# Attention-times-V of two head pairs in one excursion, their last keys as quarters of the array, two transposes moved earlier, fewer output buffers

## The chip, the cores and the metric

The kernel runs on one core of one Trainium2 chip. The metric is device time in microseconds (us), and each time quoted below for a whole kernel is a median over several executions; spans, stages and waits are read from one profiled execution. Before the change it was 528.9 us (three runs, 528.81 to 530.1). The profiled runs had a mean granted TensorE clock of 0.997 or more of full speed.

Names: PE is the TensorE matmul engine and PEld its weight loads, DVE is VectorE, ACT is ScalarE, POOL is GpSimd. PSUM is the memory into which PE accumulates; it is divided into banks, and each tile named `f` in the profile is one bank.

## The reference

```python
# q, k, v: (8, 12, 448, 64) fp32
scores = scale * (q @ k^T)                     # per batch and head, 448 x 448
attn   = maximum(scores, 0) ** 2 / 448
x      = attn @ v                              # heads side by side: (8, 448, 768)
xn     = (x - mean) / sqrt(var + 1e-6) * g_ln
out    = x + maximum(xn @ w_ch1, 0) @ w_ch2    # d_ff = 3072
```

## The kernel before

Matmuls are in bf16. The kernel works on one batch after another. While the first layer of the feed-forward of batch b runs (24 products of 12 matmuls, in halves of 64 output channels), the attention of batch b+1 is slipped in between its products as *excursions*, so that the engines that evict the scores (copy them out of PSUM) and square them have time.

Heads are handled in pairs (`i` counts pairs, 6 to a batch). The 448 keys are three tiles of 128 (`NF = 3`) and a rest of 64 (`SS`). The rest tiles of two neighbouring pairs share one tile, `attn[i, NF]` with even `i`, and its score matmuls use 64x64 quarters of the array.

The PSUM banks:

```python
sc    # 2 tiles of 2 banks: scores, evicted by ScalarE
fb    # 4 single banks
next_f = Turns(fb[:2]).next     # first-layer products AND attention-times-V take turns here
spare  = fb[2:]                 # the third score tile of an excursion, means
```

Attention-times-V (AV) of one pair goes into one bank, with eight matmuls (four tiles, two heads). The rest tile's half of V has zero rows, so all eight have the same 128x64 form:

```python
def att_AV(i, half=None, bank=None, evac_by=None):
    ...
        av[0] = (next_f() if bank is None else bank)[:, :S]
    ...
    order = [NF, 0, 1, 2] if i % 2 else [0, 1, 2, NF]
    # ... 8 matmuls into ps ...
    if evac_by is nc.scalar:
        nc.scalar.mul(xT_of(b, pr), ps, c2)                                 # eviction
    else:
        nc.vector.tensor_scalar(xT_of(b, pr), ps, c2, None, op0=Alu.mult)   # eviction
    # ... and an addition xs += xT on VectorE, for the mean
```

An excursion, and the places where it stands:

```python
def excursion(n, third=(nc.vector, nc.vector), **how):
    flush_loads()
    next_AV(**how)                              # one AV, if one is ready
    took = [slots.pop(0) for _ in range(n)]     # then n = 3 score tiles
    for m, (i, t) in enumerate(took):
        att_QK(i, t, relu_by=third if m == 2 else nc.scalar)
    for i, t in took:
        att_square(i, t)                        # VectorE, three squares
    ...
def ffn_1(ni):
    ps = next_f()[:, :S]
    # ... 12 matmuls ...
    nc.scalar.activation(h[:, ni, CARRY:], ps, Act.Relu)
# batches 1 to 6: an excursion after every third first-layer product
# (in batch 1 with evac_by=nc.scalar)
```

At the start, batch 0's own attention runs alone. Its last pair, the last two mean products (`mean_part`) and the first first-layer product on centred inputs (`ffn_1_first`) follow one another with little else to fill the gaps. The q and k of batch 1 are transposed on PE, five pairs of them inside batch 0's first layer (`T_IN_FIRST`).

## Time and profile before

| | before |
|---|---|
| median time | 528.9 us |
| span of the profiled run | 525.9 us |
| PE busy | 98% |
| chain of waits, share of PE | 81% |
| first-layer stage of batches 2 to 6, each | 37.72 us |
| first-layer stage of batch 0, batch 1 | 40.77, 39.58 us |

A *stage* here runs from its first first-layer matmul to the first second-layer matmul, by the start times of the records.

From the page of before, the span, the busy time of each engine, the granted clock in 40 slices (9 is 90% or more), and the chain that ended last, as shares of the span:

```profile
span 525.9 us, 13704 instructions
...
PE 517.0 (98%) x5705; PEld 309.9 (59%) x5705; DVE 375.3 (71%) x662; ACT 272.8 (52%) x444; POOL 221.8 (42%) x255
...
PEclk9999999999999999999999999999999999999999
...
PE 81%; DMA 12%; POOL 3%; DVE 2%; ACT 1%; issue 1%; POOLq 0%; DVEq 0%; ACTq 0%
```

TensorE bounds the kernel. To cost an edit one has to see how tightly its matmuls follow each other. The next fence is from the timeline of before, in the middle of a batch. Columns: start, duration (both us), engine, line, operation, output and input tile, shape, number of instructions, and in brackets the idle time before, with what ended it.

```profile
310.38 0.92 PE L319 MATMUL f<-at,v_ring 128*64 128x448 bf16 x8
310.65 0.54 ACT L399 ACTIVATE h<-f 128x448 bf16<-128x448 f32 x1 [0.65 <-PE f L397]
...
311.23 0.55 PE L284 MATMUL sc<-qkT_t 64*128 64x448 bf16 x4
311.42 0.62 DVE L326 TENSOR_SCALAR xT<-f 128x448 bf16<-128x448 f32 x1 [1.24 <-PE f L319]
...
311.72 0.38 PE L279 MATMUL f<-qkT_t 64*64 64x448 bf16 x4
...
312.03 3.60 PE L397 MATMUL f<-xc,w 128*64 128x448 bf16 x36
...
313.45 1.69 DVE L295 TENSOR_TENSOR at<-at 128x896 bf16<-128x896 bf16 x3
...
315.46 0.92 PE L319 MATMUL f<-at,v_ring 128*64 128x448 bf16 x8
```

Durations of matmul groups overlap the next group, because each record's end is modelled and lies about 0.35 us after its start. So one reads from start to start: 36 first-layer matmuls take 315.46 - 312.03 = 3.43 us, that is 0.19 us per pair of 128x64 halves. The AV's four pairs take 0.76 us, and to the next start it is 0.85, so the change of array tiling costs about 0.09. The AV (310.38) takes the one bank of the two, the latest first-layer product has the other. That product's ReLU runs from 310.65 to 311.19, and PE wants its bank only at 312.03, 0.84 us later. There is no hole in PE's work here.

### The profile page before, as it was taken

Reading aid. Unit: us, or ns where it says so; the run is one execution under the profiler, and the core shown is the slowest. Engines: PE = TensorE matmul, PEld = TensorE weight load, DVE = VectorE, ACT = ScalarE, POOL = GpSimd, SP = SyncE. Lnnn points to the kernel's source line nnn. Section 1 sums busy time; section 2 is a strip of 40 time slices with the busy share of each in tenths; the row PEclk is TensorE's granted clock in tenths of the full one; section 3 lists DMA queues with packets and bytes.
Section 4 is the critical chain, followed back from the end, with each engine's and each line's share of the span. In section 5 each row is a group of like instructions: output and inputs, shape, how many; then the busy total and the mean of one; then the engine's idle time right before and its main releaser. Section 6 shows DMA issues by size and latency. Waiting matters only on the chain.

```text
span 525.9 us, 13704 instructions
## 1 busy us (share of the span) xinstructions
PE 517.0 (98%) x5705; PEld 309.9 (59%) x5705; DVE 375.3 (71%) x662; ACT 272.8 (52%) x444; POOL 221.8 (42%) x255
## 2 busy tenths in 40 slices
PE   8989999999999999999999999999999999999996
PEld 4445566556765566655666556655666556665665
DVE  5967778778858869589584886788695876951265
ACT  6965551878236662366623666466524665234320
POOL 8628215676622683227732267428632000320021
PEclk9999999999999999999999999999999999999999
DMA  9999999999637993679934799769944200250022
GB/s 135 173 194 201 205 201 146 202 125 105 82 80 99 106 102 62 122 73 115 94 66 105 72 113 122 108 62 123 82 77 106 49 14 3 62 112 11 1 61 62
DMA packets 175230, 53.04 MB, mean 101 GB/s; under 512 B 154176, under 2 KB 175168, under 8 KB 175168
## 3 DMA queue, kind: packets, MB, share of 16 engines
q0 software_dynamic: 103552, 25.74, 55.3%
q1 hardware_dynamic: 71088, 26.06, 27.1%
q8 instruction: 44, 0.72, 0.6%
q10 hardware_dynamic: 528, 0.37, 0.2%
q14 instruction: 18, 0.15, 0.1%
HBM read 51.91 MB, written 11.01 MB: 120 GB/s over the span
## 4 chain that ended last, share of the span: by engine, by line
PE 81%; DMA 12%; POOL 3%; DVE 2%; ACT 1%; issue 1%; POOLq 0%; DVEq 0%; ACTq 0%
PE f L397 36%; PE f L459 34%; DMA w<-in_moe_w_ch_dram 6%; PE f L319 5%; DMA s_sb<-in_v_dram 4%; PE sc L284 3%; PE f L284 1%; DMA w<-in_k_dram 1%; DVE w L210 1%; POOL w L201 1%; PE sc L279 1%; ACT at L292 1%; POOL w L141 1%; PE f L356 0%; POOL w L144 0%
## 5 line engine op out<-in xcount | busy, mean ns | idle before, releaser
L397 PE MATMUL f<-xc,w 128*64 128x448 bf16 x2256 | 226.9, 354 | 0.7 <-DVE o_t L428 0.4
L397 PEld LDWEIGHTS <-w 128*64 128x64 bf16 x2256 | 124.6, 110 | 94.4 <-issue 19.1
L399 ACT ACTIVATE h<-f 128x448 bf16<-128x448 f32 x188 | 102.5, 545 | 102.6 <-PE f L397 101.1
L459 PE MATMUL f<-w,s_sb 128*64 128x384 bf16 (+2 forms) x1584 | 130.0, 324 | 0.0
L292 ACT ACTIVATE at<-sc 128x896 bf16<-128x896 f32 x120 | 103.4, 917 | 16.5 <-PE sc L284 13.3
L459 PEld LDWEIGHTS <-s_sb 128*64 128x64 bf16 x1584 | 89.6, 110 | 37.7
L295 DVE TENSOR_TENSOR at<-at 128x896 bf16<-128x896 bf16 x168 | 95.8, 618 | 5.1 <-ACT at L292 4.8
L166 POOL DMA_DIRECT2D qk_ring<-in_q_dram x36 | 47.0, 1305 | 95.4 <-DMA qkT_t<-qk_ring 85.9
L493 POOL TENSOR_TENSOR o_t<-o_t,x_tok 128x384 f32<-128x384 f32 x26 | 24.4, 938 | 146.6 <-ACT o_t L492 132.1
L290 DVE TENSOR_SCALAR at<-f 128x448 bf16<-128x448 f32 x89 | 51.6, 618 | 24.2 <-PE f L284 24.2
L453 DVE TENSOR_TENSOR s_sb<-h 128x1536 bf16<-128x1536 bf16 x65 | 64.8, 1014 | 0.0
L492 ACT ACTIVATE o_t<-f,rstd 128x384 f32<-128x384 f32 x26 | 15.1, 580 | 94.7 <-DVE acc L497 46.7
L167 POOL DMA_DIRECT2D qk_ring<-in_k_dram x36 | 55.2, 1533 | 9.3 <-DMA w<-in_moe_w_ch_dram 9.3
L459 PE MATMUL f<-w,h 128*64 128x384 bf16 x624 | 52.9, 326 | 0.0
L168 POOL DMA_DIRECT2D qk_ring<-in_k_dram x36 | 46.6, 1293 | 5.2 <-DMA w<-in_moe_w_ch_dram 5.2
L326 DVE TENSOR_SCALAR xT<-f 128x448 bf16<-128x448 f32 x43 | 26.7, 620 | 28.2 <-PE f L319 27.6
L459 PEld LDWEIGHTS <-h 128*64 128x64 bf16 x624 | 35.5, 110 | 15.5
L319 PE MATMUL f<-at,v_ring 128*64 128x448 bf16 x336 | 40.3, 354 | 0.5 <-DVE xT L326 0.2
L493 POOL TENSOR_TENSOR acc<-acc,x_tok 128x384 f32<-128x384 f32 x24 | 28.0, 1176 | 22.5 <-ACT acc L492 22.5
L363 DVE SCALAR_TENSOR_TENSOR xc<-f,g_sb,xc 128x448 bf16<-128x448 f32 x45 | 28.5, 678 | 6.4 <-PE f L356 6.0
L178 POOL DMA_DIRECT2D v_ring<-in_v_dram x36 | 32.3, 1202 | 0.0
L284 PE MATMUL sc<-qkT_t 64*128 64x448 bf16 x206 | 31.3, 356 | 0.0
(81 smaller groups left out, 381.1 us busy)
## 6 DMA issues: line engine op xcount, KB each, us to landing
w<-in_moe_w_ch_dram POOLq DMA_DIRECT2D x6, 768.0 KB, 12.7
w<-in_moe_w_ch_dram POOLq DMA_DIRECT2D x4, 1152.0 KB, 26.2
v_ring<-in_v_dram POOLq DMA_DIRECT2D x21, 192.0 KB, 5.4
qk_ring<-in_q_dram POOLq DMA_DIRECT2D x36, 112.0 KB, 4.7
qk_ring<-in_k_dram POOLq DMA_DIRECT2D x36, 96.0 KB, 5.2
out_dram<-o_t SPq DMA_DIRECT2D x9, 168.0 KB, 2.2
out_dram<-o_t SPq DMA_DIRECT2D x9, 144.0 KB, 2.1
out_dram<-acc SPq DMA_DIRECT2D x7, 144.0 KB, 2.0
```

What stands on the lines that cost most here:

```text
L166: nc.gpsimd.dma_start(q_to, q[b, heads].rearrange("x (p j) d -> p j x d", j=NJ))
L167: nc.gpsimd.dma_start(k_to[:, :NF], k[b, heads, :SF].rearrange("x (p t) d -> p t x d", t=NF))
L284: nc.tensor.matmul(by_j(half[hh]), k_of(i, r, t, P), q_of(i, r), start=True, stop=True)
L290: nc.vector.tensor_scalar(at[:, x], half[x], 0.0, None, op0=Alu.max)
L292: nc.scalar.activation(at, ps[:, :, :S], Act.Relu)
L295: nc.vector.tensor_mul(attn[i, t], attn[i, t], attn[i, t])
L319: nc.tensor.matmul(ps[hh * D:(hh + 1) * D, :], weights, values, start=(n == 0), stop=(n == NF))
L397: nc.tensor.matmul(ps[c * D:(c + 1) * D, :], w1[:, ki, n0:n0 + D], xc[:, ki, :], start=(ki == 0), stop=(ki == K1 - 1))
L399: nc.scalar.activation(h[:, ni, CARRY:], ps, Act.Relu)
L453: nc.vector.tensor_tensor(s_sb[:, n], x, y, op=op)
L459: nc.tensor.matmul(ps[c * D:(c + 1) * D, :d1 - d0], stat[:, ki, c * D:(c + 1) * D], w2[:, slot, ki, d0:d1], start=(start and ki == 0), sto ...
L493: nc.gpsimd.tensor_tensor(o_t, o_t, x_half(m, dh), op=Alu.add)
```

## The change

Three ideas, all meant to give PE less work or to fill its gaps.

1. AV of pairs `i` and `i+1` go into one excursion (a *joint*). Their rest tiles no longer cost two zero-padded pairs of 128x64 matmuls (0.38 us): the four 64x64 quarters run at once, in the time of one pair. The score tile that follows a joint is a rest tile in quarters too, so no further change of tiling is added. There are 14 joints, two in each of batches 0 to 6; the excursion before each goes without an AV.
2. Two of the transposes of batch 1's q and k leave batch 0's first layer for the gaps around the last two mean products.
3. The output buffers shrink (`acc` 4 to 3, `o` 3 to 2), and the attention tiles grow from 7 to 9, which the later AV needs.

```diff
+    def att_AV2(i, evac_by=None):
+        ps = [next_f()[:, :S] for _ in range(2)]
+        for x in range(2):
+            for t in range(NF):
+                av_part(ps[x], i + x, t, t == 0, False)      # three full tiles each
+        # ...
+        for x in range(2):
+            for hh in range(2):
+                r0 = row0(i + x, hh)                          # quarters
+                nc.tensor.matmul(ps[x][hh * D:(hh + 1) * D, :], v_rest[r0:r0 + SS, pr + x, r0:r0 + D],
+                                 attn[i, NF][r0:r0 + SS, x, :], start=False, stop=True)
+        for x in range(2):
+            av_out(i + x, ps[x], evac_by)
# ... in the slots:
+        if i % NPAIR == 4:
+            first[1:] = [(i, NF), (i, 1), (i, 2)]
# ... in excursion():
-        next_AV(**how)
+        if len(ready) > 1:
+            att_AV2(ready.pop(0), **how)
+            ready.pop(0)
+        elif ready and ready[0] % NPAIR == NPAIR - 2:
+            next_AV(**how)
# ... in step_fine(), for the last pairs: the square ahead of the AV's second half
# ... in first_end():
         att_AV(i - 1, 1)
+        att_T(i + 1, nc.scalar.copy, next_f())
         mean_part(i - 1)
+        att_T(i + 2, nc.scalar.copy, spare[1])
# ... in ffn_1_first():
-        tiles = [t[:, :S] for t in (f_ps, m_ps, spare[1], next_sc()[:, 0])]
+        tiles = [t[:, :S] for t in (f_ps, m_ps, next_sc()[:, 0], spare[1])]
...
-    T_IN_FIRST = {4: 1, 7: 2, 10: 3, 13: 4, 16: 5}
+    T_IN_FIRST = {10: 3, 13: 4, 16: 5}
# ... and batch 1's q and k of heads 2 to 5 are loaded before the first weight chunk
# ... buffers: attn 7 -> 9, acc 4 -> 3, o 3 -> 2
```

More of the change, by code (lines that the diff above doesn't have):

```diff
@@ L57 @@
     t_pool = ctx.enter_context(tc.tile_pool(name="qkT", bufs=3))
-    attn_pool = ctx.enter_context(tc.tile_pool(name="attn", bufs=7))
+    attn_pool = ctx.enter_context(tc.tile_pool(name="attn", bufs=9))
     st_pool = ctx.enter_context(tc.tile_pool(name="stats", bufs=4))
-    acc_pool = ctx.enter_context(tc.tile_pool(name="acc", bufs=4))
-    o_pool = ctx.enter_context(tc.tile_pool(name="o", bufs=3))
+    acc_pool = ctx.enter_context(tc.tile_pool(name="acc", bufs=3))
+    o_pool = ctx.enter_context(tc.tile_pool(name="o", bufs=2))
     ps_pool = ctx.enter_context(tc.tile_pool(name="ps", bufs=1, space=bass.MemoryType.PSUM))
@@ L248, in k_of, with att_T @@
         return flat(i)[r, c0:c0 + keys]
-    def att_T(i, copy=None):
+    def att_T(i, copy=None, bank=None):
         if i >= PE_T * NPAIR:
@@ L262, in att_T @@
             return
-        ps = bf_view(next_f() if i <= NPAIR else next_spare())
+        if bank is None:
+            bank = next_f() if i <= NPAIR else next_spare()
+        ps = bf_view(bank)
         for t in range(2):
@@ L302, in xT_of, with av_part @@
         return xT[:, ki, (b % 2) * S:(b % 2 + 1) * S]
+    def av_part(ps, i, t, start, stop):
+        b, pr = divmod(i, NPAIR)
+        v_heads, v_rest = v_parts(b)
+        for hh in range(2):
+            if t < NF:
+                weights, values = v_heads[:, 2 * pr + hh, t * D:(t + 1) * D], attn[i, t][:, hh, :]
+            else:
+                weights, values = v_rest[:, pr, row0(i, hh):row0(i, hh) + D], attn[i - i % 2, NF][:, i % 2, :]
+            nc.tensor.matmul(ps[hh * D:(hh + 1) * D, :], weights, values, start=start, stop=stop)
     def att_AV(i, half=None, bank=None, evac_by=None):
-        b, pr = divmod(i, NPAIR)
         if half != 1:
@@ L308, in att_AV, with av_out @@
         ps = av[0]
-        v_heads, v_rest = v_parts(b)
         order = [NF, 0, 1, 2] if i % 2 else [0, 1, 2, NF]
         for n, t in enumerate(order):
-            if half is not None and n // 2 != half:
-                continue
-            for hh in range(2):
-                if t < NF:
-                    weights, values = v_heads[:, 2 * pr + hh, t * D:(t + 1) * D], attn[i, t][:, hh, :]
-                else:
-                    weights, values = v_rest[:, pr, row0(i, hh):row0(i, hh) + D], attn[i - i % 2, NF][:, i % 2, :]
-                nc.tensor.matmul(ps[hh * D:(hh + 1) * D, :], weights, values,
-                                 start=(n == 0), stop=(n == NF))
-        if half == 0:
-            return
+            if half is None or n // 2 == half:
+                av_part(ps, i, t, n == 0, n == NF)
+        if half != 0:
+            av_out(i, ps, evac_by)
+    def att_AV2(i, evac_by=None):
[3 more added lines that the diff above has]
+                av_part(ps[x], i + x, t, t == 0, False)
+        b, pr = divmod(i, NPAIR)
+        v_rest = v_parts(b)[1]
+        for x in range(2):
+            for hh in range(2):
+                r0 = row0(i + x, hh)
[3 more added lines that the diff above has]
+            av_out(i + x, ps[x], evac_by)
+    def av_out(i, ps, evac_by):
+        b, pr = divmod(i, NPAIR)
         if evac_by is nc.scalar:
@@ L412, in new_o, with new_acc @@
         return o_t
+    def new_acc():
+        acc_t = acc_pool.tile([P, HD], fp32, tag="acc")
+        return acc_t
     def store(o_t, m, d0, d1, engines=(nc.sync,)):
@@ L444, in plain_part @@
         if part == parts - 1:
-            o_t = acc_pool.tile([P, HD], fp32, tag="acc")
+            o_t = new_acc() if dh else new_o()
             scaled_plus(o_t, box[m], m, x_half(m, dh))
@@ L476, in seven @@
         bb = c
-        acc1 = acc_pool.tile([P, HD], fp32, tag="acc")
-        acc2 = acc_pool.tile([P, HD], fp32, tag="acc")
+        acc1, acc2 = new_acc(), new_acc()
         tt = nc.vector.tensor_tensor
@@ L552, in after @@
                 def after(ps=ps, d0=d0, d1=d1):
-                    o_t = new_o()[:, :d1 - d0]
-                    scaled_plus(o_t, ps[:, :d1 - d0], m2, acc2[:, d0:d1])
+                    o_t = acc2[:, d0:d1]
+                    scaled_plus(o_t, ps[:, :d1 - d0], m2, o_t)
                     store(o_t, m2, HD + d0, HD + d1, (nc.sync, nc.scalar))
@@ L581 @@
             first[2:] = first[:1:-1]
-        slots += first + [(i + 1, t) for t in range(NF)]
+        second = [(i + 1, t) for t in range(NF)]
+        if i % NPAIR == 4:
+            first[1:] = [(i, NF), (i, 1), (i, 2)]
+        slots += first + second
     slots = slots[slots.index((NPAIR, 2)):]
@@ L588, in ends @@
         if i % 2 == 0:
-            return [i] if t == (NF - 1 if i % NPAIR == 2 else NF) else []
+            return [i] if t == (NF - 1 if i % NPAIR else NF) else []
         return [i] if t == NF - 1 else []
@@ L597, in excursion @@
         flush_loads()
-        next_AV(**how)
+        if len(ready) > 1:
+            assert ready[0] % 2 == 0 and ready[1] == ready[0] + 1
+            att_AV2(ready.pop(0), **how)
+            ready.pop(0)
+        elif ready and ready[0] % NPAIR == NPAIR - 2:
+            next_AV(**how)
         took = [slots.pop(0) for _ in range(n)]
@@ L640, in step_fine @@
             mean_part(i - 1)
-        att_AV(i, 1)
-        att_square(i + 1, 2)
+        if i + 2 < NPAIR:
+            att_AV(i, 1)
+            att_square(i + 1, 2)
+        else:
+            att_square(i + 1, 2)
+            att_AV(i, 1)
     def first_end():
@@ L783 @@
         load_heads(1, [("q", 0, 2), ("k", 0, 2), ("k last", 0, H)])
+        load_heads(1, [("q", 2, 4), ("k", 2, 4)])
         load_w1(0)
-        load_heads(1, [("q", 2, 4), ("k", 2, 4)])
         load_w1(1)
```

## The prediction

> **What bounds it.** TensorE. The page has PE busy 98% of 525.9 us, granted clock full; the chain of waits is 81% PE. In batches 2 to 6 the timeline shows PE without holes: 36 first-layer matmuls start 3.43 us apart from the next stage (0.19 us per pair of 128x64 halves), AV takes 0.76 us (four pairs), a change of array tiling costs 0.09 to 0.13 us. (The Trainium skill, "TensorEngine Tiling (Array Packing)", Key Properties, says that changing the mode drains the engine; the trace agrees, with those numbers.) From AV to AV an excursion lasts 4.96 or 5.08 us. PE is stalled elsewhere: 0.7 us before the last mean product, 0.8 us before the first centred product, and some tenths per excursion in batch 1 (ScalarE late).
>
> **Removed.** Two AV of a joint excursion take 6 pairs plus one set of four quarters (four 64x64 score matmuls go out in 0.19 us) instead of 8 pairs: -0.19 us, 14 times, -2.7 us. No tiling change is added, since quarter scores now follow directly. Two transposes leave the first-layer loop, 0.61 us each: -1.2 us.
>
> **Added, by the order of instructions.**
> (a) The second AV takes the PSUM bank that the first-layer product just before used. Its ReLU ends 0.81 us after AV starts (ScalarE starts 0.27 us after, takes 0.54); PE would want the bank after 0.57 us. Matmuls are served in order (the Trainium skill, "TensorE: Matmul & The Clock Gate", Part 3: MATMULs strict FIFO), so PE stands: estimate +0.29 us per joint excursion.
> (b) Both first-layer banks now hold AV, so the next first-layer product waits for VectorE: it starts 0.47 us after the last AV matmuls, takes 0.62; scores between cover some 0.98. Estimate +0.17 us.
> (c) In the second joint excursion VectorE has one more eviction and one more addition (0.62 and 0.39 us) ahead of the squares; the following AV, one excursion later, then waits for its third tile: estimate +0.27 us per batch.
> So per batch 2 to 6: 2 x (-0.19+0.29+0.17)+0.27 = +0.8 us, +4.0 in all. Stage of batch 0, the same: +0.8. Batch 1 evicts on ScalarE, which is already late: two evictions before the score ReLUs put the next first-layer ReLU off; estimate: a pair of excursions 11.1, not 10.4 us, +1.5 in all.
> (d) Start: the transposes fill the two stalls, but the square now goes ahead of AV's eviction, so the last mean product comes about 0.4 us later, and the fourth tile of the first product waits about 0.35 us for ScalarE's transpose copy (some 0.9 us). Net -0.4. The first weight chunk lands about 28.8 us (24.35 before), still ahead of its use at 29.8.
> Fewer output buffers: free; their reuse is over 7 us apart, and a store lands in 2.
>
> **Sum.** -0.4+0.8+1.5+4.0 = about +5.9 us; a little discounted, 534.2 us, range 528.5 to 538. Chances: faster by over 2% 0.01, within 2% 0.93, slower by over 2% 0.06.
>
> **Signs.** Right: PE idle before the second AV's first matmuls until a first-layer ReLU, and before the next first-layer product until VectorE's xT, about 14 times each; two excursions (without and with AV) 10.3 us against 10.04; batch 1's stage about 1.5 us longer. Wrong: joint excursions with no such gaps, quarters slower than 0.2 us, or the first centred product after 31 us.
>
> **What would make it wrong.** ReLU or eviction earlier than I read: then up to 3.5 us faster, 525. Quarters that don't run together, or the late first weight chunk: slower.

## The result, and the profile after

The changed kernel took 534.12 us (median of 4, 533.36 to 535.01), against 528.86 us for the kernel before in the same rounds (median of 4, 528.25 to 530.1). The ratio is 1.0097, with a 95% interval of 1.0073 to 1.0121. Ratios here are the mean time of one kernel's fast runs over that of the other's in the same rounds, so they are not quite the ratio of the medians.

From the page of after:

```profile
span 533.2 us, 13735 instructions
...
PE 519.6 (97%) x5705; PEld 315.4 (59%) x5705; DVE 373.8 (70%) x660; ACT 272.6 (51%) x446; POOL 222.5 (42%) x255
...
PEclk9999999999999999999999999999999999999999
...
PE 73%; DMA 11%; DVE 6%; ACT 4%; POOL 3%; issue 2%; ACTq 0%; POOLq 0%; DVEq 0%
```

The number of matmuls is the same, 5705. PE's busy share hardly moves, and its busy time even rises by 2.6 us although the change takes work off it. What moves is the chain: PE falls from 81% to 73%, DVE rises from 2% to 6% and ACT from 1% to 4%. PE now waits more often for the engines that evict its results.

From the timeline of after, the excursion with a joint AV and the next one:

```profile
311.18 3.60 PE L419 MATMUL f<-xc,w 128*64 128x448 bf16 x36
...
314.42 0.68 PEld L314 LDWEIGHTS <-v_ring 128*64 128x64 bf16 x7
314.61 1.62 PE L314 MATMUL f<-at,v_ring 128*64 128x448 bf16 x12
...
314.87 0.54 ACT L421 ACTIVATE h<-f 128x448 bf16<-128x448 f32 x1 [0.59 <-PE f L419]
315.47 0.33 PEld L314 LDWEIGHTS <-v_ring 128*64 128x64 bf16 x5 [0.38 <-issue]
...
316.16 0.38 PE L338 MATMUL f<-at,v_ring 64*64 64x448 bf16 x4
...
316.37 0.36 PE L281 MATMUL sc<-qkT_t 64*64 64x448 bf16 x4
...
316.65 0.62 DVE L348 TENSOR_SCALAR xT<-f 128x448 bf16<-128x448 f32 x1 [2.31 <-PE f L338]
316.66 0.36 PE L286 MATMUL sc<-qkT_t 64*128 64x448 bf16 x2
...
316.86 0.35 PE L286 MATMUL f<-qkT_t 64*128 64x448 bf16 x2
...
317.31 0.39 DVE L357 TENSOR_TENSOR xs<-xs,xT 128x448 bf16<-128x448 bf16 x1
317.33 3.60 PE L419 MATMUL f<-xc,w 128*64 128x448 bf16 x36
...
317.62 0.62 DVE L348 TENSOR_SCALAR xT<-f 128x448 bf16<-128x448 f32 x1
...
319.64 1.68 DVE L297 TENSOR_TENSOR at<-at 128x896 bf16<-128x896 bf16 x3
...
320.73 1.22 PE L314 MATMUL f<-at,v_ring 128*64 128x448 bf16 x8
...
321.88 0.55 PE L286 MATMUL sc<-qkT_t 64*128 64x448 bf16 x4
```

Three things are to be seen, and they are the waits (a), (b) and (c) of the prediction.

- **(a)** The joint starts at 314.61. Its quarters start at 316.16, 1.55 us later, though six pairs at 0.19 us and a tiling change should take about 1.23. The weight loads show where the hold is: seven, a pause of 0.38 us, and five more from 315.47. The pause ends just after the ReLU (314.87 + 0.54 = 315.41), which read the bank that the second AV needs.
- **(b)** The two last pairs of score matmuls start at 316.66 and 316.86. The next first-layer product starts at 317.33, 0.67 us after the first of them; where nothing holds it, as in the experiment without quarters below, that is 0.49. VectorE's eviction of the first AV ends at 316.65 + 0.62 = 317.27, and its bank is the one that this product takes.
- **(c)** The AV of the next excursion starts at 320.73 and the scores after it at 321.88: 1.15 us for eight matmuls that took 0.85 in before. Its third tile is the last of VectorE's three squares, which end at 319.64 + 1.68 = 321.32; the first matmul on that tile starts at 321.38. They end late because VectorE has two evictions and two additions ahead of them.

The same read over the whole trace gives the following, from the start times of the PE records:

| | before | after | predicted difference |
|---|---|---|---|
| second AV after the first | - | 0.80 to 0.89 us, one of 1.14 | (a) +0.29 over an unhindered 0.57 |
| second-to-last score pair, to the next first-layer product | 0.49 (in `e3`) | 0.66, 12 times of 14 | (b) +0.17 |
| single AV after a joint's excursion | 0.86 | 1.15, six times | (c) +0.27 |
| pair of excursions, without and with AV | 10.04 | 306.98 to 317.33 = 10.35 | 10.3 |

The two joints without (b) are those of batch 1's stage, where ScalarE evicts.

By stage, in the profiled runs (us):

| stage | before | after | difference |
|---|---|---|---|
| up to the first first-layer matmul | 29.79 | 29.93 | +0.14 |
| first layer, batch 0 | 40.77 | 41.50 | +0.73 |
| second layer, batch 0 | 15.98 | 16.42 | +0.44 |
| first layer, batch 1 | 39.58 | 41.01 | +1.43 |
| first layer, batches 2 to 6 | 5 x 37.72 | 38.49, 38.88, 38.60, 38.61, 38.61 | +4.60 |
| all others | | | 0.0 |

They sum to +7.3 us, which is the difference of the two spans. The medians differ by 5.3. The profiled run of before happened to be one of its fastest (527.67 us) and that of after its slowest (535.01), so of the stages that scatter from run to run (the start and batch 0) not all is the change's.

How little of this the wait view tells is worth a look. From the waits of PE of after (waited-for, us in total, times, longest):

```profile
PE f L229 <- DMA w<-in_k_dram: 1.0, 1, 1.0
...
PE f L419 <- ACT h L421: 0.9, 2, 0.5
...
PE f L314 <- ACT h L421: 0.4, 1, 0.4
```

For wait (a) it lists one entry of 0.4 us, where reading from start to start finds 14 waits of 0.24 us or more (0.803 less 0.567). The holds are there as idle time, but in small pieces. A pair of matmuls lasts 0.35 us by its records and the next pair normally starts after 0.19, so some 0.17 us of each hold lie under the record before it. What is left, read record by record from the kept trace, is a gap of 0.06 to 0.13 us before the second AV (13 times; the 14th is the 0.41 of the list) and of 0.11 us before the next first-layer product (12 times). The wait view of these runs lists nothing under 0.2 us. The page adds such gaps up: the idle time before the matmuls of a line is its last column. For the AV and the first-layer products, before and after:

```profile
L319 PE MATMUL f<-at,v_ring 128*64 128x448 bf16 x336 | 40.3, 354 | 0.5 <-DVE xT L326 0.2
L397 PE MATMUL f<-xc,w 128*64 128x448 bf16 x2256 | 226.9, 354 | 0.7 <-DVE o_t L428 0.4
...
L314 PE MATMUL f<-at,v_ring 128*64 128x448 bf16 x288 | 37.0, 355 | 2.5 <-ACT h L421 0.4
L419 PE MATMUL f<-xc,w 128*64 128x448 bf16 x2256 | 226.7, 353 | 3.3 <-ACT h L421 0.9
```

(The Trainium skill, "Perfetto Trace Analysis", Tensor Engine Instruction, says that the profiler estimates the end of a TensorE record rather than observing it. This trace agrees: PE's busy time went up from 517.0 to 519.6 us although the change takes work off it, so part of the holds is counted as busy. Of the 7.3 us by which the span grew, 4.7 are idle and 2.6 busy.)

The first line of the wait view is a wait that is large enough to show, and it is new: the third transpose of batch 1 (the first that is left in batch 0's first layer) stands at 44.82 us, 1.9 earlier than in before (46.69), and waits 1.0 us for its k to land.

### The profile page after: what moved, and what is told of

It is laid out like the page before. It is cut to its first block, busy times and chain, and to the rows that moved or that the text cites. A ratio compares the mean times of both kernels' runs of the same rounds, so it can differ in the third digit from the quotient of the medians.

```text
span 533.2 us, 13735 instructions
## 1 busy us (share of the span) xinstructions
PE 519.6 (97%) x5705; PEld 315.4 (59%) x5705; DVE 373.8 (70%) x660; ACT 272.6 (51%) x446; POOL 222.5 (42%) x255
## 4 chain that ended last, share of the span: by engine, by line
PE 73%; DMA 11%; DVE 6%; ACT 4%; POOL 3%; issue 2%; ACTq 0%; POOLq 0%; DVEq 0%
PE f L485 33%; PE f L419 31%; DMA qk_ring<-in_q_dram 6%; DMA s_sb<-in_v_dram 4%; PE f L314 3%; PE sc L286 2%; ACT h L421 2%; DVE xT L348 2%; DVE at L297 2%; ACT at L294 1%; DMA w<-in_q_dram 1%; DVE at L292 1%; DVE w L210 1%; PE f L286 1%; PE f L338 1%
## 5 line engine op out<-in xcount | busy, mean ns | idle before, releaser
L419 PEld LDWEIGHTS <-w 128*64 128x64 bf16 x2256 | 131.9, 110 | 92.6 <-issue 21.6
L294 ACT ACTIVATE at<-sc 128x896 bf16<-128x896 f32 x120 | 103.3, 917 | 22.6 <-PE sc L281 16.4
L485 PEld LDWEIGHTS <-s_sb 128*64 128x64 bf16 x1584 | 89.4, 110 | 37.9
L166 POOL DMA_DIRECT2D qk_ring<-in_q_dram x36 | 45.3, 1259 | 93.5 <-DMA qkT_t<-qk_ring 71.1
L167 POOL DMA_DIRECT2D qk_ring<-in_k_dram x36 | 54.1, 1502 | 9.4 <-DMA w<-in_moe_w_ch_dram 9.4
L168 POOL DMA_DIRECT2D qk_ring<-in_k_dram x36 | 45.0, 1251 | 5.7 <-DMA w<-in_moe_w_ch_dram 5.7
L314 PE MATMUL f<-at,v_ring 128*64 128x448 bf16 x288 | 37.0, 355 | 2.5 <-ACT h L421 0.4
L518 POOL TENSOR_TENSOR acc_t<-acc_t,x_tok 128x384 f32<-128x384 f32 x24 | 28.9, 1212 | 22.6 <-ACT acc_t L517 22.6
L178 POOL DMA_DIRECT2D v_ring<-in_v_dram x36 | 33.6, 1268 | 0.0
L286 PE MATMUL sc<-qkT_t 64*128 64x448 bf16 x192 | 30.0, 356 | 0.0
```

The lines of the kernel that those rows point to most:

```text
L166: nc.gpsimd.dma_start(q_to, q[b, heads].rearrange("x (p j) d -> p j x d", j=NJ))
L167: nc.gpsimd.dma_start(k_to[:, :NF], k[b, heads, :SF].rearrange("x (p t) d -> p t x d", t=NF))
L286: nc.tensor.matmul(by_j(half[hh]), k_of(i, r, t, P), q_of(i, r), start=True, stop=True)
L294: nc.scalar.activation(at, ps[:, :, :S], Act.Relu)
L314: nc.tensor.matmul(ps[hh * D:(hh + 1) * D, :], weights, values, start=start, stop=stop)
L419: nc.tensor.matmul(ps[c * D:(c + 1) * D, :], w1[:, ki, n0:n0 + D], xc[:, ki, :], start=(ki == 0), stop=(ki == K1 - 1))
```

## The experiments

The theory: PE lost three waits' worth in each batch, (a) for ScalarE's ReLU, (b) for VectorE's eviction and (c) for VectorE's squares; the quarters themselves do what they should. The rivals: the moved transposes and loads at the start, or the smaller buffers, cost the time; or the quarters do not run together, or their tiling changes cost more than they save. All ten kernels gave correct results, with five rounds each (five or six runs of the kernel, eleven of the one before). The kernel before had medians of 528.45 us (the runs of the first group, up to `e4`), 528.5 (`e5` to `e7`) and 528.24 (`e8` to `e10`).

Stages by experiment (us, profiled runs), to be looked up from the texts below:

| kernel | up to first layer | batch 0 | batch 1 | batches 2 to 6, each | median | ratio to before |
|---|---|---|---|---|---|---|
| before | 29.79 | 40.77 | 39.58 | 37.72 | 528.86 | 1 |
| after | 29.93 | 41.50 | 41.01 | 38.5 to 38.9 | 534.12 | 1.0097 |
| e1 | 29.35 | 41.55 | 41.01 | 38.5 to 38.6 | 533.9 | 1.0106 |
| e2 | 30.2 | 39.53 | 39.87 | 37.7 | 527.79 | 0.9991 |
| e3 | 29.8 | 40.26 | 40.59 | 37.9 to 38.3 | 529.55 | 1.0021 |
| e4 | 29.58 | 40.80 | 40.08 | 37.98 | 529.99 | 1.0027 |
| e5 | 29.85 | 40.83 | 39.90 | 38.18 | 531.23 | 1.0056 |
| e6 | 30.61 | 41.17 | 40.12 | 37.66 | 528.23 | 0.9999 |
| e7 | 30.53 | 41.02 | 40.20 | 37.66 | 528.59 | 0.9991 |
| e8 | 29.86 | 40.44 | 40.48 | 37.39 | 525.8 | 0.9952 |
| e9 | 29.09 | 41.98 | 38.81 | 37.39 | 524.93 | 0.9935 |
| e10 | 29.88 | 39.20 | 38.82 | 37.39 | 524.58 | 0.9928 |

### e1_start_undone: the change without its new start

```diff
-            att_square(i + 1, 2)       # for the last pairs
-            att_AV(i, 1)
+            att_AV(i, 1)
+            att_square(i + 1, 2)
...
-        att_T(i + 1, nc.scalar.copy, next_f())
         mean_part(i - 1)
-        att_T(i + 2, nc.scalar.copy, spare[1])
...
-    T_IN_FIRST = {10: 3, 13: 4, 16: 5}
+    T_IN_FIRST = {4: 1, 7: 2, 10: 3, 13: 4, 16: 5}
# and the order of tiles and of loads as before
```

> The change without its new start (transposes, order of loads, square before AV put back; the joint AV and the buffers kept). If the joint AV costs all of the 5.3 us, as I read the trace (three new waits of PE), this stays at about 534 us (533 to 535.5), with AV gaps as in the changed kernel. If the start is to blame (first weight chunk late, a new wait of 1.0 us for k), this comes near 530 us.

Measured: 533.9 us (533.55 to 535.39), ratio 1.0106 (1.0088 to 1.0124). The loss is all still there, so the new start did not cause it. It did not measurably help either.

### e2_joint_undone: the change without its joints

The AV, the slots and the excursion are those of before; the new start and the buffer counts are those of the change.

```diff
-        if len(ready) > 1:
-            att_AV2(ready.pop(0), **how)
-            ready.pop(0)
-        elif ready and ready[0] % NPAIR == NPAIR - 2:
-            next_AV(**how)
+        next_AV(**how)
# and att_AV, slots and ends as before
```

> The change without the joint AV (AV of one pair per excursion and the old order of slots put back; new start and new buffers kept). Joint AV to blame: about 528.7 us (527.5 to 529.5), no PE gap in batches 2 to 6. Start or buffers to blame: 531 us or more.

Measured: 527.79 us (527.35 to 529.32), ratio 0.9991 (0.9974 to 1.0009). The whole loss goes with the joints. The smaller output buffers and the new start, taken together, are free. Batches 2 to 6 are back at 37.71 to 37.75 us.

### e3_no_quarters: joints, but with the zero-padded rest tile

```diff
         for x in range(2):
-            for t in range(NF):
-                av_part(ps[x], i + x, t, t == 0, False)
-        # ... the quarters
+            for t in range(NF + 1):
+                av_part(ps[x], i + x, t, t == 0, t == NF)
```

> The change with the last keys of the two pairs on the whole array again, one pair after the other: PE has 14 x 0.19 = 2.7 us more of matmuls. Waits to blame: the first pair ends before the second begins, is evicted earlier, and the wait for the eviction goes; the wait for the ReLU shrinks from 0.3 to 0.1 us: so it is FASTER than the change by some 3 to 4 us, about 530.5 us (529.5 to 532). If the work on PE decides, or quarters only bring what they save: about 536.8 us.

Measured: 529.55 us (529.17 to 530.04), ratio 1.0021 (1.0004 to 1.0037). This kernel gives PE more work than the change, by 14 x 0.19 = 2.7 us, and is 4.4 us faster than `e1`, which has the change's joints and ran in the same rounds. From its timeline, PE only:

```profile
311.40 1.81 PE L314 MATMUL f<-at,v_ring 128*64 128x448 bf16 x16
313.14 0.38 PE L281 MATMUL sc<-qkT_t 64*64 64x448 bf16 x4
313.45 0.36 PE L286 MATMUL sc<-qkT_t 64*128 64x448 bf16 x2
...
313.94 3.60 PE L412 MATMUL f<-xc,w 128*64 128x448 bf16 x36
317.37 0.92 PE L314 MATMUL f<-at,v_ring 128*64 128x448 bf16 x8
318.22 0.55 PE L286 MATMUL sc<-qkT_t 64*128 64x448 bf16 x4
```

The two AV take 1.74 us to the next start: eight pairs are 1.52, and the rest is the tiling change and what remains of (a). The first-layer product comes 0.49 us after the scores at 313.45, so (b) is gone, and the next AV takes 0.85, so (c) is gone. The reason can be read off: with its fourth tile in place, the first AV keeps PE busy 0.19 us longer before the second bank is wanted, and it closes its accumulation before the second AV begins, so VectorE can start evicting it early. The quarters put the close of both AV at the very end. The second AV starts 0.80 to 0.89 us after the first (once 1.14) in this kernel as in the change: the work that the quarters remove in front of wait (a) only lengthens the wait.

It does not mean that the quarters fail to run together. Four of them go out in 316.37 - 316.16 = 0.21 us in the change, nearly as fast as one pair of full tiles (0.19).

### e4_own_bank: take away (a)

The first-layer product right before a joint writes into a spare bank, so the second AV's bank was free long before.

```diff
-    def ffn_1(ni):
-        ps = next_f()[:, :S]
+    def ffn_1(ni, bank=None):
+        ps = (next_f() if bank is None else bank)[:, :S]
...
-            ffn_1(ni)
+            joint = {0: (11, 17), 1: (12, 18), B - 1: ()}.get(b, (10, 16))
+            ffn_1(ni, spare[1] if ni in joint else None)
```

> The change, with the first-layer product just before each joint excursion put into another, idle bank, so that the second AV's bank has long been free; nothing else moves. Bank theory: the wait for the ReLU, about 0.3 us each of 14 times, goes, the wait for the eviction (0.18 us) stays: about 530.0 us (529.3 to 531). If the gap before the second AV has another cause (weights, tiling): no change, 534 us.

Measured: 529.99 us (528.86 to 530.67), ratio 1.0027 (1.0009 to 1.0045). From its timeline, PE only:

```profile
310.81 1.30 PE L314 MATMUL f<-at,v_ring 128*64 128x448 bf16 x12
312.04 0.38 PE L338 MATMUL f<-at,v_ring 64*64 64x448 bf16 x4
...
312.55 0.36 PE L286 MATMUL sc<-qkT_t 64*128 64x448 bf16 x2
...
313.21 3.60 PE L419 MATMUL f<-xc,w 128*64 128x448 bf16 x36
```

The quarters come 1.23 us after the joint's start, 14 times of 14, where the change had 1.49 or more. A batch of 2 to 6 falls from 38.61 to 37.98 us, 0.31 per joint: that is (a). Wait (b) is still 313.21 - 312.55 = 0.66, and (c) is still 1.16. A new wait appeared in batch 1: the quarter scores stood 0.5 us for transposed q and k that had not landed.

### e5_act_first: take away (b)

ScalarE evicts the joint's first AV, VectorE the second.

```diff
         for x in range(2):
-            av_out(i + x, ps[x], evac_by)
+            av_out(i + x, ps[x], (nc.scalar, nc.vector)[x])
```

> The change with one edit: of a joint excursion's two AV, the first is evicted by ScalarE and the second by VectorE, in all batches. If the next first-layer product waits for VectorE's eviction, that wait (0.18 us, 12 times) goes; if the next excursion's AV waits because VectorE has an eviction more ahead of its squares, that one (0.29 us, 6 times) goes too; batch 1, which evicted both on ScalarE, gains up to 0.4 us per joint excursion. The wait for the ReLU before the second AV stays. About 529.3 us (528.5 to 531). If neither wait is VectorE's: 534 us, or more, as ScalarE has more to do.

Measured: 531.23 us (530.18 to 532.8), ratio 1.0056 (1.0038 to 1.0073). From its timeline, PE only:

```profile
312.93 0.38 PE L338 MATMUL f<-at,v_ring 64*64 64x448 bf16 x4
...
313.43 0.36 PE L286 MATMUL sc<-qkT_t 64*128 64x448 bf16 x2
...
313.94 3.60 PE L419 MATMUL f<-xc,w 128*64 128x448 bf16 x36
```

Wait (b) is gone: 313.94 - 313.43 = 0.51, against 0.66. A batch of 2 to 6 is 38.18, against 38.61. That is 0.21 per joint, more than (b)'s 0.15, because the second AV now starts 0.80 us after the first in all of them, where in batches 3 to 6 of the change it was 0.86; in batch 2, where it was 0.80 in the change too, the gain is (38.49 - 38.18) / 2 = 0.155. The expectation had (c) go as well and so asked for more; that was a miss. The AV after a joint still took 1.15 us. One eviction less did not suffice: VectorE still had the second eviction and both additions ahead of its squares, and the first addition, which comes before its own eviction in program order, now waited for ScalarE's (it starts at 313.92 us, and the view names ScalarE's eviction as what ended 3.01 us of idle time before it). Counted from the joint's start, the squares end after 6.51 us against 6.71 in the change, and the AV that needs them starts after 5.90 against 6.12: both come about 0.2 us earlier, so the wait stayed.

### e6_both: own bank and ScalarE first

Both edits, as above.

> The two cures together: own bank for the first-layer product before a joint excursion, first eviction on ScalarE. If the three waits are the whole cost, what is left is the saved 0.19 us per joint excursion: stages of batches 2 to 6 at about 37.35 us against 37.72 in the kernel before, and in all about 526.3 us (525.3 to 527.3), faster than both kernels. If the quarters or the joint form cost something of their own, it stays at 528.5 us or more.

Measured: 528.23 us (527.17 to 530.34), ratio 0.9999 (0.9978 to 1.002). Batches 2 to 6 take 37.66 us, less than before's 37.72, and the loss is gone. The expectation of a gain was missed, for two reasons. Wait (c) stayed, as in `e5`. And PE, which now reached batch 1 earlier, met the loads. From the timeline of this kernel, in batch 1:

```profile
107.45 0.35 PE L281 MATMUL sc<-qkT_t 64*64 64x448 bf16 x2
108.98 0.38 PE L281 MATMUL sc<-qkT_t 64*64 64x448 bf16 x2 [1.18 <-DMA qkT_t<-qk_ring]
```

Two of the four quarter scores wait 1.18 us for a transposing DMA. In batch 0 it also waited 1.1 us for k and 0.9 us for the first weight chunk.

### e7_both_qk_first: load batch 1's last q and k before its v

```diff
-        load_heads(1, [("v", 0, H), ("v last", 0, H), ("q", 6, 6), ("k", 6, 6)])
+        load_heads(1, [("q", 6, 6), ("k", 6, 6), ("v", 0, H), ("v last", 0, H)])
```

> As the run before, with the last q and k of batch 1 loaded ahead of that batch's v. The transposes that stood 0.8 to 1.0 us waiting for that k in the traces with the new start then find it there; the v come later, some 46 us, just before the first joint AV. About 0.5 us less than the run before (0 to 1.0). If the first joint AV now waits for v instead: no gain.

Measured: 528.59 us (525.28 to 529.04), ratio 0.9991 (0.9969 to 1.0014). No gain, a miss. The wait for k is gone, but PE then stands 1.4 us for a weight chunk, before the product at 50.98 us. The edit did not make that chunk late: it landed at 50.94 us, and at 51.14 in `e6`, where PE came to it just in time because it had stood for k before (its first joint started at 48.97 us, here at 47.29). So two waits stood one behind the other, and taking the first away only bared the second. (The other waits of this profile, 1.0 us for the first weight chunk, which was 0.9 in `e6`, 0.3 for the next, and 0.5 for v at 11.4 and 17.4 us, come before the moved q, k and v are used.) The wait for transposed q and k in batch 1 stayed at 1.2 us.

### e8_cured_old_start: also take away (c), with the start of before

Built on `e1`, with the edits of `e4` and `e5`, and two for (c): VectorE's additions for the mean run after the squares, and the next AV uses its rest tile second, so that its freshest tile comes last.

```diff
-        order = [NF, 0, 1, 2] if i % 2 else [0, 1, 2, NF]
+        order = [NF, 0, 1, 2] if i % 2 else [0, NF, 1, 2] if i % NPAIR == 4 and b else [0, 1, 2, NF]
...
-            nc.vector.tensor_add(xs, xs, xT_of(b, pr))
+            adds.append((xs, xT_of(b, pr)))
...
         for i, t in took:
             att_square(i, t)
+        run_adds()
```

> The joint AV with the start of the kernel before and three cures: own bank, first eviction on ScalarE, and VectorE's additions put behind the squares, with the next AV taking its last-squared tile last. If the 0.29 us that the runs with one or two cures still show before that AV are its wait for the squares, stages of batches 2 to 6 take 37.35 us (37.66 with two cures, 37.72 before). Whole kernel: batch 1 still waits about 1 us for transposed q and k, so about 526.5 us (525.5 to 527.5). If that gap isn't the squares': 37.66 us, 528 us.

Measured: 525.8 us (525.21 to 527.09), ratio 0.9952 (0.9936 to 0.9967), faster than before by 2.4 us. Batches 2 to 6 take 37.39 us each, 0.27 less than in `e6`: that is (c), and with it the third wait is shown. The two edits for it were not tried apart. The wait for transposed q and k in batch 1 was 1.5 us.

### e9_cured_late_v: two loads of v later

```diff
-    V_AT = {21: PE_T * NPAIR + 2, 23: PE_T * NPAIR + 4}    # in batch 0's first layer
+    V_AT = {7: PE_T * NPAIR + 2, 10: PE_T * NPAIR + 4}     # in batch 1's
...
-            if b == 0 and ni in V_AT:
+            if b == 1 and ni in V_AT:
```

> As the run before, with two loads of v moved from the end of batch 0's stage into batch 1's, behind the loads of q and k that batch 1's first joint excursion needs. If its wait for q and k (1.2 us in the trace with two cures) comes from standing behind these v, it goes or shrinks: about 1 us less than the run before, 525.5 us (524.5 to 526.7), and no wait of PE for transposed q and k. Otherwise no gain.

Measured: 524.93 us (524.69 to 525.77), ratio 0.9935 (0.9922 to 0.9949). Batch 1's stage falls from 40.48 to 38.81 us and the wait for q and k is no longer listed: the transposes that it stood for landed at 105.31 and 106.16 us, against 108.18 and 109.02 in `e8`. So what made q and k late was the v ahead of them. (Batch 0's stage of this profiled run, 41.98 us against 40.44 in `e8`, is no effect of the edit. From 29.4 us on the granted clock was one half for 3.4 us, and matmuls of the first product started 0.37 us apart where they take 0.19.) From its timeline, a joint with all three waits cured:

```profile
308.54 1.30 PE L314 MATMUL f<-at,v_ring 128*64 128x448 bf16 x12
...
309.77 0.38 PE L339 MATMUL f<-at,v_ring 64*64 64x448 bf16 x4
...
310.19 0.54 ACT L347 ACTIVATE xT<-f 128x448 bf16<-128x448 f32 x1 [0.90 <-PE f L339]
...
310.79 3.60 PE L426 MATMUL f<-xc,w 128*64 128x448 bf16 x36
...
314.19 0.95 PE L314 MATMUL f<-at,v_ring 128*64 128x448 bf16 x8
...
315.07 0.55 PE L286 MATMUL sc<-qkT_t 64*128 64x448 bf16 x4
```

Quarters 1.23 us after the start, first-layer product at 310.79 with ScalarE's eviction done at 310.73, next AV in 0.88 us. A pair of excursions, without and with AV, lasts 9.87 us (300.92 to 310.79 by the starts of the first-layer products), against 10.04 in before and 10.35 in the change.

### e10_cured_new_start: all of it, with the change's start

`e9` with the start of the change (the diff of `e1` the other way round).

> As the run before, with the change's start. In traces with the new start the first weight chunk landed at 26.2, 29.4 and 30.6 us, against its use at 29.8, and PE waited up to 1.1 us for k later; with the old start neither. If the start's gain of 1.2 us is given back so, this is within 1 us of the run before, either way: 525 us (524 to 526.7), with more scatter. If the start is worth its transposes: 1.2 us less.

Measured: 524.58 us (523.67 to 525.56), ratio 0.9928 (0.9912 to 0.9945). It is the fastest of the twelve, 3.7 us below before and 9.5 below the change, if one compares medians over different rounds. Against `e9` of the same rounds it is 0.35 us better by the medians, with overlapping ranges, so the new start is worth little. (The stages of the two profiled runs differ by more, but `e9`'s has the stretch of halved clock in it; at 525.77 us it was its slowest run.) How much of this is the joint's own? `e2`, which has the same start and no joint, had 527.79, some 3 us more, but in other rounds and without the later v. In batches 2 to 6, where these do not come in, the cured joints give 5 x (37.72 - 37.39) = 1.65 us.

## Why the prediction was right, and where it was off

The class, the size and the mechanism held: 534.2 us predicted with a range of 528.5 to 538, 534.12 measured. That the number was met within 0.1 us is luck in part: the terms summed to +5.9 us and were discounted without a stated reason, the start was mis-sized (below), and four runs of one kernel spread over 1.9 us (528.25 to 530.1).

- **What bounds it.** Right. TensorE does, and its in-order queue passes every hold on to all that follows. (The Trainium skill, "TensorE: Matmul & The Clock Gate", Part 3, says that matmuls start and end in program order, "strict FIFO, no reordering". The trace agrees: while the second AV waits in the change, up to 315.47 us, the scores behind it wait too, although their q and k had landed by 312.63 and the ReLU that frees their bank had ended by 312.83.)
- **Removed, -0.19 us per joint.** Right. Cured, a batch takes 37.39 us against 37.72 in before, -0.33 for two joints or -0.17 each.
- **(a) +0.29 per joint.** Right: +0.24 to +0.32 by the second AV's start (0.80 to 0.89 less 0.57), 0.31 by what `e4` gained.
- **(b) +0.17 per joint.** Right: 0.15 to 0.18 at the wait itself, 0.155 by `e5` in batch 2. (In the other batches `e5` gained 0.21, but there wait (a) shrank too.)
- **(c) +0.27 per batch.** Right: 0.29 at the AV itself, 0.27 by `e6` against `e8`. The prediction named VectorE's addition with the eviction; the expectation of `e5` left it out, and missed.
- **Batches 2 to 6, +4.0 us.** +4.6 measured in the profiled run. **Batch 1, +1.5**: +1.43, and by the path that was named: its two joints start 11.09 us apart (106.57 and 117.66; predicted 11.1), and PE waits twice for ScalarE's first-layer ReLU, 0.5 us each. In `e5`, where ScalarE evicts one AV of the two, these waits are gone and the stage is 39.90 us.
- **(d) Start, -0.4, and batch 0, +0.8.** Batch 0's joints were right: `e1`, which has them with the old start, takes 41.55 us in that stage, +0.78. The start is the term that was mis-sized. It changed by +0.14 up to the first first-layer matmul, and the transposes did take 1.2 us out of batch 0's stage, but 1.0 us came back as a wait of the third transpose for k, which the prediction did not foresee: with two transposes (1.22) and one AV (0.86) gone ahead of it, the third comes 1.9 us earlier and is there before its data. So the start's term is about +0.14 - 1.22 + 1.01 = -0.1, not -0.4, in this run. The wait depends on when the load lands: `e10`, with the same start and joints, shows none. The second layer of batch 0 added 0.44 that was not foreseen either; that stage was 15.98 or 16.3 to 16.4 us in different kernels and runs, with the old start and with the new, so it may be scatter. The first weight chunk, predicted at 28.8, landed at 29.38 in the change, and between 26.0 and 30.6 in the other kernels with the new start. In `e6` and `e7` it was late enough to hold PE for about 1 us.
- **The signs to look for.** The prediction said that the gaps would show as idle PE about 14 times each. They do, 14 and 12 times, but as gaps of mostly 0.06 to 0.13 us, which the wait view leaves out: it lists (a) once, 0.4 us. A reader who had looked there only could have called the mechanism wrong; the idle column of the page, 2.5 us for 0.5 and 3.3 for 0.7, and the start times show it.
- **Fewer output buffers.** Free, as said, as far as `e2` can tell: it has them together with the new start, and no loss (0.9974 to 1.0009).

What was not foreseen at all is that the waits can be cured: the prediction took the idea for a losing one, and it is a gaining one (0.9928) once each of the two AV has a bank of its own in time and an engine that evicts it.

Still open: why one joint in the profiled run waited longer than the others (1.14 us between its AV; its ReLU came 0.28 us late, and the same joint of `e3` has the same 1.14), the scatter of the first weight chunk, the 0.4 us in the second layer of batch 0, and the share of each of the two edits that cured (c).

## What to carry to other kernels

When two results are put where one was, count banks and evictions as well as matmuls: which bank the second result takes and who last reads it, when each accumulation closes, and what the evicting engine has to do first. Taking work off the bounding engine directly ahead of a wait gained nothing here, since the wait grew by as much. On a pipelined engine look for small waits from start to start, because part of each hold lies under the modelled record before it and the wait view may list nothing of the rest.

## What the Trainium skill lacked or had wrong

- "TensorEngine Tiling (Array Packing)", Key Properties, says that changing the tiling mode drains the engine, without a figure. Here a change cost about 0.09 us (128x64 to 64x128) to 0.13 us. Quarters of one product followed by quarters of another needed none: 0.21 us from start to start, against 0.19 from one pair of halves to the next.
- "Perfetto Trace Analysis", Identifying the Most-Contended Engine, warns of matmul busy time as a measure of roofline. It does not say that idle time understates a hold of PE as well: of 14 holds of 0.24 us or more, about 0.17 us each lie under the record before, 13 leave gaps of 0.06 to 0.13 us, and the wait view lists one of 0.4. The pauses in the weight loads (0.38 us) and the start times show them.
- "PSUM — Partial Sum Buffer", PSUM bank collisions, has the rule to guard PSUM by semaphores, by bank and quadrant or simply by bank, but no page gives what the two hand-overs of a bank take; the skill's costs are those of the matmul and of the evicting instruction alone. Here, for 448 fp32 columns of a bank: from the last AV pair's start to VectorE's eviction 0.47 us (0.12 after the end of its record), and from the eviction's end to the next matmul into the bank about 0.06 us (317.27 to 317.33). The eviction between them took 0.62 us on VectorE or 0.54 on ScalarE.
